# A two-layer decode step: layer 1's FFN gate and up products formed as rows, the last down product formed as rows on top of x, and more unread products between the layers

## The chip, the cores and the metric

The kernel runs on one core of a Trainium2 chip. The core has five engines with queues of their own: TensorE (matrix products, results to the PSUM banks), VectorE, ScalarE, GpSimd and SyncE (which here issues all transfers from HBM to SBUF). They run at the same time and wait for each other only through semaphores. The metric is the device time of one execution in microseconds (us); lower is better. Three runs of the kernel before took 645.3, 645.9 and 646.07 us, so the median is 645.9 us.

## The reference, cut to what matters

Two identical layers act on 4 sequences with one new token each. The weights and the caches are the same ones in both layers, so each layer needs all of the K and V cache.

```python
B, Sq, D = 4, 1, 512;  Hq, Hkv, Sk, Dh = 32, 8, 8192, 128;  F = 1792

def _A_ref(x, k_cache, v_cache, wq, wo):            # attention with 4 query heads per KV head
    q = (x @ wq).reshape(B, Sq, Hq, Dh).transpose(0, 2, 1, 3)
    k = jnp.repeat(k_cache, 4, axis=1);  v = jnp.repeat(v_cache, 4, axis=1)
    scores = jnp.einsum("bhqd,bhkd->bhqk", q, k) * (Dh ** -0.5)
    o = jnp.einsum("bhqk,bhkd->bhqd", _softmax(scores), v)
    return o.transpose(0, 2, 1, 3).reshape(B, Sq, Hq * Dh) @ wo

def _B_ref(x, w_gate, w_up, w_down):                # SwiGLU FFN
    return (_silu(x @ w_gate) * (x @ w_up)) @ w_down

x = x + _A_ref(_layernorm(x), ...);  x = x + _B_ref(_layernorm(x), ...)    # layer 1
x = x + _A_ref(_layernorm(x), ...);  x = x + _B_ref(_layernorm(x), ...)    # layer 2
```

K and V are 128 MiB together, in bfloat16.

## The kernel before, in words

**Units and slots.** The cache is cut into 32 units per layer, one for each sequence and KV head. K of a unit is 2 MB and so is V. SBUF has eight slots of this size; a transfer for a later unit is issued as soon as the unit that held the slot is done with it (`finished`, `pump`), all on SyncE's queue. Most units come as one transfer; those around the border between the layers come in quarters of 512 KB (`part`). K and V of the last three units of layer 1 stay in six slots and are used first in layer 2. In the meantime the other two slots (6 and 7) and a small extra area hold the FFN weights: w_gate (4 pieces of 448 KB), w_up (4 pieces, read once and kept for layer 2), w_down (7 pieces of 256 KB, one for each pair of 128 rows).

**Attention of a unit.** VectorE turns K in 32x32 blocks (`turn`), TensorE forms the scores in 8 blocks of 4 products of 256 columns (`scores`). Then five steps wait in a list `line` and are put between other work at estimated distances: `max_p` (VectorE), `max_t` (TensorE transpose, VectorE maximum, ScalarE copy), `exps` (TensorE broadcast of the maximum, ScalarE exponential), `turn_p`, `total`. `values` then multiplies by V, 16 products of 512 columns that go to four column groups of TensorE (lines 598 to 604). The last unit of a layer takes another form (`block_last`), eight blocks of 8 products of 32 columns, each waiting for its quarter of V. At the end of a KV head `out_proj` multiplies by wo and `add_to_x` adds to x. The scores, V products and softmax steps of the next or previous units are interleaved in the order in which Python calls them; each engine executes its own queue strictly in that order (`T.tape`).

**The border.** After the last unit of layer 1: `center` (the norm: sums by a product with ones, subtraction, squares), then `ffn(False)`, then `center` again, `qmul` (q of layer 2's first head), `qcast`, `qpick`, `place_q` and the first scores. All on x of 128 partitions by 16 columns, so every step is short and hands over between TensorE and VectorE.

**The FFN before.** w_gate and w_up are multiplied as weights: for each of 4 pieces (kt), 14 products with a 128x128 block as the stationary operand and 4 columns of x, repeated to 32, as the moving one (lines 782 to 789). The deviation of the norm comes in the middle of the gate. `gr`, `eg`, `gw` form silu on 128x56 (lines 793 to 799), and `hT` multiplies by up (line 800). w_down goes the same way, 14 x 4 products (lines 807 to 810). In layer 1, SyncE gets the first three K quarters of layer 2 (into slot 6) after the gate products, and four more after the second, sixth, tenth and last group of w_down, as the weights are used up (lines 790 to 792 and 811 to 817).

**The first unit of layer 2.** Its K is in a kept slot. After every second of its eight score blocks the slot's quarter is free and a V quarter of a later unit is issued into it (`quarter`, lines 559 to 563). So these transfers wait for TensorE's scores.

**The end.** Layer 2's FFN reads x plus the down product into `xn` (line 819). Four transposes on TensorE bring it to rows, ScalarE and VectorE copy one half each, and SyncE writes the 4 KB of output (lines 909 to 921).

**Unread products.** `warm(n, k)` (line 693) issues products of a wq block with itself, n pieces of 256 columns, into a bank that nobody reads. They depend on nothing late and fill time in which TensorE would wait.

Of the kernel before, what the change touches and what calls it, by code (L numbers as in the profile page):

```python
# [5 lines left out]
ACTF = mybir.ActivationFunctionType  # L6
# [139 lines left out]
def bass_interleave_layers__gqa_block_cached__swiglu_ffn__decode_kernel(  # L146
# [18 lines left out]
    P = 128  # L165
# [25 lines left out]
    with ExitStack() as es:  # L191
# [61 lines left out]
        def bank(k):  # L253
            return ps[:, k * BANKF:(k + 1) * BANKF]
# [162 lines left out]
        def part(it, s, a, b, sem_):  # L417
            kind, L, u = it
            assert (L, u) in fours
            n = NB // NQ  # L420
            w, m = n * TB * Dh, S // NQ
            src = (A_k_cache if kind == "K" else A_v_cache)[u % B, u // B, :, :]
            T.dma("sp", [(kv[:, s, q * w:(q + 1) * w], runs(src[q * m:(q + 1) * m, :])) for q in range(a // n, b // n)],
                  sem_, writes=[f"s{s}.{k}" for k in range(a, b)])

        def place(it, s):
            assert items[issued[0]] == it
            slot_of[it] = s
            issued[0] += 1
# [151 lines left out]
        def values(L, u):  # L581
            g, b = unit_gb(u)
            bk = OBK[turn_of[u]]
            def begin():
                flush(line, u)
                flush(after, turn_of[u])
# [5 lines left out]
            def block(i):  # L592

                if i == 0:
                    begin()
                s = slot_of["V", L, u]
                v = kv[:, s, :].rearrange("p (q t d) -> p t q d", t=TB, d=Dh)
                for t in range(TB):
                    j = t % NA
                    c0 = t * QB + i * NV * REP  # L600
                    T.pe(bank(bk)[j * QB:j * QB + NV * REP, :], pT[:, turn_of[u], c0:c0 + NV * REP],
                         v[:, t, NV * i:NV * (i + 1), :],
                         reads=[f"s{s}.{NV * i + k}" for k in range(NV)] + [f"pT{turn_of[u]}"], writes=[f"pb{bk}"],
                         sig=(t == TB - 1), start=(i == 0 and t == j), stop=(i == 1 and t >= TB - NA))
                if i == 1:
                    end()
# [158 lines left out]

        def ffn(last):
            gb, ub = OBK
            gT = bank(gb)[:, 0:FO * B]
            uT = bank(ub)[:, 0:FO * B]
            fb = lambda ap: ap.rearrange("p (f b) -> p f b", b=B)  # L770
            rb = rstd[:].unsqueeze(1).to_broadcast([P, FO, B])
            ks = items[ends[0] + 1:ends[0] + 3]
            n = NB // NQ
            w6 = KT * F // (TB * Dh) // n * n
            for (w_sb, wname, bk) in (([wg_sb[:, k, :] for k in range(KT)], "wg", gb), (wu_sb, "wu", ub)):
                out = bank(bk)[:, 0:WIDE // B * FO * B].rearrange("p (r f b) -> p f r b", f=FO, b=B)
# [13 lines left out]
                if bk == gb and not last:  # L790
                    place(ks[0], NKEEP)
                    part(ks[0], NKEEP, 0, w6, sem_p[0])
            T.op("dve", lambda e: e.tensor_tensor(fb(gr), fb(gT), rb, ALU.mult),
                 reads=[f"pb{gb}", "rstd"], writes=["gr"])
            T.op("act", lambda e: e.activation(eg, gr, ACTF.Exp, scale=-1.0), reads=["gr"], writes=["eg"])
            T.op("dve", lambda e: e.tensor_tensor(fb(gw), fb(gr), rb, ALU.mult), reads=["gr", "rstd"], writes=["gw"])
# [3 lines left out]
            T.op("dve", lambda e: e.tensor_tensor(hT, eg, uT, ALU.mult), reads=[f"pb{ub}", "eg"], writes=["hT"])  # L800
            out = bank(OUTB)[:, 0:WIDE // B * XB].rearrange("p (r n b) -> p n r b", n=KT, b=B)
            for fo in range(FO):
                if not last:
                    warm(2 if fo % 2 == 0 else 0)
                elif fo in (0, FO - 4, FO - 2):
                    warm(3 if fo == 0 else 1)
                for nt in range(KT):
                    T.pe(out[:, nt, :, :], wd_sb[:, fo, nt * P:(nt + 1) * P], few(hT[:, fo * B:(fo + 1) * B]),
                         start=(fo + nt == 0), stop=(fo == FO - 1 and nt == KT - 1),
                         reads=["hT"] + at_w["wd", fo // 2], writes=[f"pb{OUTB}"], sig=(nt == KT - 1 and fo % 2 == 1))  # L810
                if not last and (f1 - f0 + (fo + 1) * D) % (n * TB * Dh) == 0:
# [6 lines left out]
            if last:  # L818
                T.op("dve", lambda e: e.tensor_tensor(xn[:], xT[:], bank(OUTB)[:, 0:XB], ALU.add),
                     reads=["x", f"pb{OUTB}"], writes=["xn"])  # L820
            else:
                add_to_x()


        def roll(name):
# [57 lines left out]
        for L in range(2):  # L883
            turn_of.update((u, i % 2) for i, u in enumerate(unit_order[L]))
            rl_of.update((u, i % CYCLE) for i, u in enumerate(unit_order[L]))
            center(2 * L)
            first = unit_order[L][0] // B
            qmul(first)
            warm(L)
            qcast()  # L890
            qpick()
            warm(L)
            place_q(unit_order[L][0], "dve", ob4, [f"pb{OUTB}"])
            qkeep()
# [12 lines left out]
            ffn(L == 1)  # L907

        warm(2)
        for i, (k, eng, copy) in enumerate(((LNB, "act", lambda e, a, b: e.activation(a, b, ACTF.Copy)),  # L910
                                            (TOT, "dve", lambda e, a, b: e.tensor_copy(a, b)))):
            a, n = i * D // 2, KT // 2
            for kt in range(i * n, (i + 1) * n):
                T.pe(bank_bf(k)[0:B, kt * P:(kt + 1) * P], xn[:, kt * B:(kt + 1) * B], ident,
                     is_transpose=True, start=True, stop=True,
                     reads=["xn", "ident"], writes=[f"pb{k}"], sig=(kt == (i + 1) * n - 1))
            T.op(eng, lambda e: copy(e, xio[:, a:a + D // 2], bank_bf(k)[0:B, a:a + D // 2]), reads=[f"pb{k}"],
                 writes=[SCR[i]])
# [33 lines left out]
```

## Time and profile before

| what | value |
|---|---|
| median of three runs | 645.9 us |
| the profiled execution, its own time | 645.87 us |
| its span, first to last instruction | 644.1 us |
| busy: TensorE products, VectorE, ScalarE, GpSimd | 512.3, 448.8, 119.2, 19.3 us |
| mean granted clock of TensorE | 0.907 |
| bytes read from HBM | 273.42 MB |
| w_up's four pieces, when the products that wait for them start | 340.76, 341.83, 342.92, 344.00 us |
| layer 1's hT written, its last w_down pair started | 344.56, 348.39 us |
| layer 2's first scores | 351.51 us |
| output issued | 642.52 us |

The span is 1.8 us shorter than the time, which also holds what lies before the first and after the last instruction. Busy times of different engines lie beside each other and don't add up. A product's row includes the time in which its results drain from the array, so products that follow each other overlap in the rows. "Granted clock" is the share of TensorE's full clock that it was given in a stretch; 0.50 means that every product streams at half speed. The DMA share is the mean share of time in which the 16 DMA engines had a packet in work.

### The profile page before, as it was taken

Reading aid. Unit: us, or ns where it says so; the run is one execution under the profiler, and the core shown is the slowest. Engines: PE = TensorE matmul, PEld = TensorE weight load, DVE = VectorE, ACT = ScalarE, POOL = GpSimd, SP = SyncE. Lnnn points to the kernel's source line nnn. Section 1 sums busy time; section 2 is a strip of 40 time slices with the busy share of each in tenths; the row PEclk is TensorE's granted clock in tenths of the full one; section 3 lists DMA queues with packets and bytes.
Section 4 is the critical chain, followed back from the end, with each engine's and each line's share of the span. In section 5 each row is a group of like instructions: output and inputs, shape, how many; then the busy total and the mean of one; then the engine's idle time right before and its main releaser. Section 6 shows DMA issues by size and latency. Waiting matters only on the chain.

```text
span 644.1 us, 13095 instructions
## 1 busy us (share of the span) xinstructions
PE 512.3 (80%) x5088; PEld 333.1 (52%) x5113; DVE 448.8 (70%) x1105; ACT 119.2 (19%) x396; POOL 19.3 (3%) x73
## 2 busy tenths in 40 slices
PE   1657796877968877696988888989978878888887
PEld 1424464544535644454655655656555545555555
DVE  2646666866866866868763739889776776768783
ACT  0111121211211211211221222122221221111221
POOL 0000000000000000000000000000000000000000
PEclk9976789987999798889899989899798799869899
DMA  8999999999999999999999999999999999999996
GB/s 356 425 446 418 431 434 440 428 423 444 432 427 436 440 427 425 438 433 429 433 418 420 399 442 422 437 428 433 433 429 436 429 436 431 436 431 429 428 426 289
DMA packets 12744, 273.76 MB, mean 425 GB/s; under 512 B 3048, under 2 KB 3056, under 8 KB 3056
## 3 DMA queue, kind: packets, MB, share of 16 engines
q1 hardware_dynamic: 12720, 273.44, 99.1%
q8 instruction: 16, 0.26, 0.2%
q14 instruction: 8, 0.07, 0.0%
HBM read 273.42 MB, written 0.00 MB: 425 GB/s over the span
## 4 chain that ended last, share of the span: by engine, by line
DMA 63%; PE 19%; DVE 13%; SPq 2%; issue 1%; ACT 1%; DVEq 0%; POOL 0%; POOLq 0%
DMA kvf<-in_A_k_cache_dram 48%; PE ps L99 19%; DMA kvf<-in_A_v_cache_dram 11%; DVE kvf L117 8%; DMA kvf<-in_B_w_down_dram 3%; DVE acc L117 2%; SPq L135 2%; DVE one L117 1%; DVE pT L117 1%; DVE m L117 1%; ACT pb L117 0%; DVE oT L117 0%; DVEq L867 0%; ACT acc L117 0%; DVE qg L117 0%
## 5 line engine op out<-in xcount | busy, mean ns | idle before, releaser
L117 DVE STREAM_TRANSPOSE kvf<-kvf 128x512 f32<-128x512 f32 x488 | 322.5, 685 | 85.4 <-DMA kvf<-in_A_k_cache_dram 85.4
L99 PE MATMUL ps<-kvf,zq 128*128 128x256 bf16 x2048 | 314.7, 295 | 17.6 <-DVE kvf L117 12.3
L99 PEld LDWEIGHTS ps<-kvf,zq 128*128 128x128 bf16 x2048 | 196.1, 107 | 80.3 <-DVE kvf L117 30.0
L117 ACT ACTIVATE pb<-m 1x128 f32<-1x128 f32 x64 | 19.7, 308 | 438.6 <-DVE m L117 438.6
L99 PE MATMUL ps<-kvf,pT 128*16 128x512 bf16 x992 | 66.8, 391 | 11.5 <-DVE rl L117 6.9
L117 DVE SCALAR_TENSOR_TENSOR acc<-ps,own,acc 128x128 f32<-128x128 f32 x186 | 65.1, 350 | 6.2 <-ACT acc L117 1.5
L99 PE MATMUL ps<-identf,one 128*1 128x128 f32 x64 | 17.5, 274 | 50.3 <-DVE one L117 50.1
L99 PEld LDWEIGHTS ps<-identf,one 128*1 128x1 f32 x64 | 5.1, 80 | 78.5 <-DVE one L117 75.4
L99 PEld LDWEIGHTS ps<-kvf,pT 128*16 128x16 bf16 x992 | 19.3, 89 | 41.0 <-issue 21.4
L117 DVE TENSOR_REDUCE one<-ps 128x1 f32<-128x256 f32 x64 | 26.0, 406 | 18.3 <-PE ps L99 18.0
L99 PE MATMUL ps<-head,acc 128*128 128x4 f32 x124 | 23.9, 263 | 16.1 <-DVE acc L117 16.1
L117 ACT ACTIVATE pb<-ps,one,rstd 128x256 bf16<-128x256 f32 x64 | 36.1, 564 | 2.1
L99 PEld LDWEIGHTS ps<-head,acc 128*128 128x128 f32 x124 | 21.7, 218 | 28.0 <-DVE acc L117 27.0
L487 POOL TENSOR_TENSOR zq<-scr,quad 128x64 bf16<-128x64 bf16 x62 | 18.2, 293 | 600.3 <-PE ps L99 473.7
L99 PEld LDWEIGHTS ps<-one,pb 1*128 1x128 f32 x128 | 21.5, 209 | 27.0 <-ACT pb L117 21.8
L99 PE MATMUL ps<-one,pb 1*128 1x1 f32 x128 | 26.9, 277 | 9.5 <-ACT pb L117 9.5
L117 DVE RECIPROCAL rl<-ps 128x4 f32<-128x4 f32 x64 | 10.4, 162 | 33.3 <-PE ps L99 33.3
L99 PE MATMUL ps<-wq_sb 128*128 128x512 bf16 (+1 forms) x92 | 28.0, 369 | 2.7 <-issue 0.9
L117 DVE STREAM_TRANSPOSE pT<-pb 128x256 bf16<-128x256 bf16 x64 | 26.0, 407 | 4.4 <-ACT pb L117 4.3
L99 PE MATMUL ps<-xn,wq_sb 128*128 128x32 bf16 x270 | 19.8, 182 | 7.0 <-DMA wq_sb<-in_A_wq_dram 6.2
L99 PEld LDWEIGHTS ps<-o,wo_sb 128*128 (+1 forms) x256 | 20.4, 100 | 7.6 <-issue 3.5
L99 PE MATMUL ps<-o,wo_sb 128*128 128x32 bf16 x256 | 23.9, 181 | 0.1
(65 smaller groups left out, 245.4 us busy)
## 6 DMA issues: line engine op xcount, KB each, us to landing
kvf<-in_A_k_cache_dram SPq DMA_DIRECT2D x56, 2048.0 KB, 29.0
kvf<-in_A_v_cache_dram SPq DMA_DIRECT2D x56, 2048.0 KB, 32.6
kvf<-in_A_k_cache_dram SPq DMA_DIRECT2D x20, 512.0 KB, 9.0
kvf<-in_A_v_cache_dram SPq DMA_DIRECT2D x20, 512.0 KB, 11.2
wq_sb<-in_A_wq_dram SPq DMA_DIRECT2D x4, 1024.0 KB, 8.6
wo_sb<-in_A_wo_dram SPq DMA_DIRECT2D x8, 512.0 KB, 37.1
kvf<-in_B_w_gate_dram SPq DMA_DIRECT2D x8, 448.0 KB, 17.9
kvf<-in_B_w_down_dram SPq DMA_DIRECT2D x14, 256.0 KB, 18.5
```

What stands on the lines that cost most here:

```text
L99: return e.matmul(out, lhsT=lhsT if at is None else lhsT(place(at)), rhs=rhs, **kw)
L117: self.tape[engname].append((repr((name, args, kw)), lambda e, _: getattr(e, name)(*args, **kw), left, sig, None))
L135: ins = e.add_instruction(mybir.InstDMACopy(name=self.nc.get_next_instruction_name(), mode="Copy", queue="qSPDynamicHW", ins=e.lower_ap_dm ...
L487: T.op(eng, lambda e: e.tensor_tensor(dst, q4, m4_, ALU.mult), reads=keys_ + ["quad"], writes=["zq"])
```

## The change

It has four parts.

1. In `values`, when the next-to-last unit of a layer begins its V products, the list `line` is first run down to two entries. So `max_p`, `max_t` and `exps` of the last unit stand ahead of these products on every queue, in both layers.
2. `ffn(False)`: gate and up are formed as rows. For each piece, four products take x's 4 columns as the stationary operand and 448 columns of the weights as the moving one; the four go to the column groups at partitions 0, 32, 64 and 96 of one bank. When a matrix is done, VectorE turns the bank's 448 columns in 32x32 blocks from one PSUM bank into another (gate to the first score bank, up to the gate's bank), and `gT`, `uT` read every 32 columns' first four. The silu's first three operations (`gates`) stand right behind the gate's turn; the rest stands behind up's turn. Unread products: two pieces before each gate piece but the first, five before each up piece (before: three before all but up's first), six before the first w_down group (before: two).
3. `ffn(True)`: w_down is formed as rows. Two banks take 256 output columns each. Four products with the f32 identity put x there first, then for each of the 14 blocks two products with hT's 4 columns as the stationary operand and 256 columns of w_down as the moving one, at partitions 0 and 32. The addition, the four transposes and the unread products between w_down's groups are gone; ScalarE and VectorE copy the two row halves from PSUM.
4. At the border `center`, `qmul` and `qpick` of layer 2 get more unread products: four, three, two and three pieces where there were three, two, one and one.

```diff
             def block(i):
                 if i == 0:
+                    if u == unit_order[L][-2]:
+                        while len(line) > 2:
+                            line.pop(0)[2]()
                     begin()
...
-            gT = bank(gb)[:, 0:FO * B]
-            uT = bank(ub)[:, 0:FO * B]
+            gk, uk = (gb, ub) if last else (SBK[0], gb)
+            gT, uT = (bank(k)[:, 0:FO * (B if last else QB)].rearrange("p (f x) -> p f x", f=FO)[:, :, 0:B] for k in (gk, uk))
...
+            def gates():
+                T.op("dve", lambda e: e.tensor_tensor(fb(gr), gT, rb, ALU.mult),
+                     reads=[f"pb{gk}", "rstd"], writes=["gr"])
+                T.op("act", lambda e: e.activation(eg, gr, ACTF.Exp, scale=-1.0), reads=["gr"], writes=["eg"])
+                T.op("dve", lambda e: e.tensor_tensor(fb(gw), fb(gr), rb, ALU.mult), reads=["gr", "rstd"], writes=["gw"])
...
                 for kt in range(KT):
+                    if not last:
+                        if bk == gb and kt == KT // 2:
+                            deviation(zero_sb, "zero")
+                        if bk == ub or kt:
+                            warm(5 if bk == ub else 2)
+                        for j in range(NA):
+                            T.pe(bank(bk)[j * QB:j * QB + B, 0:F // NA], xn[:, kt * B:(kt + 1) * B],
+                                 w_sb[kt].rearrange("p (a j y) -> p a j y", j=NA, y=2 * QB)[:, :, j, :],
+                                 start=(kt == 0), stop=(kt == KT - 1), reads=at_w[wname] + [f"{wname}{kt}", "xn"],
+                                 writes=[f"pb{bk}"], sig=(j == NA - 1 and kt == KT - 1))
+                        continue
...
-                    if bk == ub and kt and not last:
-                        warm(3)
...
+                if not last:
+                    to = (SBK[0], gb)[bk == ub]
+                    T.op("dve", lambda e: e.transpose(bank(to)[:, 0:F // NA], bank(bk)[:, 0:F // NA].rearrange(
+                        "p (a i e) -> p a e i", e=2, i=QB)), reads=[f"pb{bk}"], writes=[f"pb{to}"])
+                    if bk == gb:
+                        place(ks[0], NKEEP)
+                        part(ks[0], NKEEP, 0, w6, sem_p[0])
+                        gates()
+            if last:
+                gates()
             T.op("dve", lambda e: e.tensor_scalar(eg, eg, 1.0, None, op0=ALU.add), reads=["eg"], writes=["eg"])
             T.op("dve", lambda e: e.reciprocal(eg, eg), reads=["eg"], writes=["eg"])
             T.op("dve", lambda e: e.tensor_tensor(eg, gw, eg, ALU.mult), reads=["gw", "eg"], writes=["eg"])
...
+            if last:
+                rows = [bank(k)[i * QB:i * QB + B, 0:D // 2] for i, k in enumerate((OUTB, STEP))]
+                for kt in range(KT):
+                    i, j = kt // (KT // 2), kt % (KT // 2)
+                    T.pe(rows[i][:, j * P:(j + 1) * P], xT[:, kt * B:(kt + 1) * B], identf[:], start=(j == 0), stop=False,
+                         reads=["x", "ident"], writes=[f"pb{(OUTB, STEP)[i]}"], sig=False)
+                warm(1)
+                for fo in range(FO):
+                    for i in range(2):
+                        T.pe(rows[i], hT[:, fo * B:(fo + 1) * B], wd_sb[:, fo, i * D // 2:(i + 1) * D // 2],
+                             start=False, stop=(fo == FO - 1), reads=["hT"] + at_w["wd", fo // 2],
+                             writes=[f"pb{(OUTB, STEP)[i]}"], sig=(fo == FO - 1))
+                return rows
...
-                if not last:
-                    warm(2 if fo % 2 == 0 else 0)
-                elif fo in (0, FO - 4, FO - 2):
-                    warm(3 if fo == 0 else 1)
+                warm(6 if fo == 0 else 2 if fo % 2 == 0 else 0)
...
-            center(2 * L)
+            center(3 * L)
...
-            warm(L)
+            warm(2 * L)
...
-            warm(L)
+            warm(3 * L)
...
-        warm(2)
...
+        T.op("act", lambda e: e.activation(xio[:, 0:D // 2], rows[0], ACTF.Copy), reads=[f"pb{OUTB}"], writes=[SCR[0]])
+        T.op("dve", lambda e: e.tensor_copy(xio[:, D // 2:D], rows[1]), reads=[f"pb{STEP}"], writes=[SCR[1]])
```

More of the change, by code (lines that the diff above doesn't have):

```diff
@@ L789, in ffn @@
                              sig=(fo == FO - 1 and kt == KT - 1))
[L790 to L796, printed above, removed]
+                if not last:
[8 more added lines that the diff above has]
+                gates()
             T.op("dve", lambda e: e.tensor_scalar(eg, eg, 1.0, None, op0=ALU.add), reads=["eg"], writes=["eg"])
@@ L799, in ffn @@
             T.op("dve", lambda e: e.tensor_tensor(eg, gw, eg, ALU.mult), reads=["gw", "eg"], writes=["eg"])
-            T.op("dve", lambda e: e.tensor_tensor(hT, eg, uT, ALU.mult), reads=[f"pb{ub}", "eg"], writes=["hT"])
+            T.op("dve", lambda e: e.tensor_tensor(fb(hT), fb(eg), uT, ALU.mult), reads=[f"pb{uk}", "eg"], writes=["hT"])
+            if last:
[11 more added lines that the diff above has]
+                return rows
             out = bank(OUTB)[:, 0:WIDE // B * XB].rearrange("p (r n b) -> p n r b", n=KT, b=B)
             for fo in range(FO):
-                if not last:
-                    warm(2 if fo % 2 == 0 else 0)
-                elif fo in (0, FO - 4, FO - 2):
-                    warm(3 if fo == 0 else 1)
+                warm(6 if fo == 0 else 2 if fo % 2 == 0 else 0)
                 for nt in range(KT):
@@ L810, in ffn @@
                          reads=["hT"] + at_w["wd", fo // 2], writes=[f"pb{OUTB}"], sig=(nt == KT - 1 and fo % 2 == 1))
-                if not last and (f1 - f0 + (fo + 1) * D) % (n * TB * Dh) == 0:
+                if (f1 - f0 + (fo + 1) * D) % (n * TB * Dh) == 0:
                     i = (f1 - f0 + (fo + 1) * D) // (n * TB * Dh) - NQ
@@ L817, in ffn @@
                         part(ks[1], NKEEP + 1, (i - 1) * n, i * n, sem_p[1 + i])
[L818 to L822, printed above, removed]
+            add_to_x()
         def roll(name):
@@ L906, in bass_interleave_layers__gqa_block_cached__swiglu_ffn__decode_kernel @@
             center(3)
-            ffn(L == 1)
-        warm(2)
[L910 to L918, printed above, removed]
+            rows = ffn(L == 1)
+        T.op("act", lambda e: e.activation(xio[:, 0:D // 2], rows[0], ACTF.Copy), reads=[f"pb{OUTB}"], writes=[SCR[0]])
+        T.op("dve", lambda e: e.tensor_copy(xio[:, D // 2:D], rows[1]), reads=[f"pb{STEP}"], writes=[SCR[1]])
         T.wait_res("sp", reads=SCR)
```

## The prediction

> **What bounds the kernel now.** First the page: the DMA row and the queue's share.
>
> ```profile
> DMA  8999999999999999999999999999999999999996
> q1 hardware_dynamic: 12720, 273.44, 99.1%
> HBM read 273.42 MB, written 0.00 MB: 425 GB/s over the span
> ```
>
> One queue keeps the 16 DMA engines busy for 99.1% of the span. No product can finish before its bytes are there, so an edit to a compute engine can change the time in two ways only: by letting the queue run dry, or by changing what follows the last byte. I looked for both.
>
> For the first, the stages around the border between the layers (columns: stretch, its length, then busy PE, PEld, DVE, ACT, POOL, granted clock, DMA share, GB/s):
>
> ```profile
> 344.80:348.30 3.50, 3.26 (x53) 1.75 (x54) 0.00 (x0) 0.00 (x0) 0.00 (x0) 1.00 1.08 442
> 348.30:351.70 3.40, 2.70 (x49) 1.61 (x50) 1.48 (x9) 0.15 (x1) 0.00 (x0) 1.00 0.98 414
> 351.70:355.10 3.40, 3.40 (x19) 2.46 (x18) 1.90 (x3) 2.20 (x4) 0.00 (x0) 0.50 1.01 424
> 355.10:358.50 3.40, 2.90 (x27) 2.25 (x25) 1.47 (x3) 0.00 (x0) 0.29 (x1) 1.00 0.94 352
> ```
>
> The clock is 0.50 for exactly the 3.4 us in which layer 2's first scores run, after 3.4 us of short work (norm, q). Right after, the DMA drops to 352 GB/s. From 354 to 362 the same view gives 381 GB/s against 429 in an undisturbed 10 us (590 to 600): 8 x (1 - 381/429) = 0.90 us of transfer lost. SyncE's timeline and the DMA issues (size, then us to landing), asked for in narrow windows, show why:
>
> ```profile
> 340.61 8.65 SPq L135 DMA_DIRECT2D kvf<-in_A_k_cache_dram  x7
> 353.58 2.18 SPq L135 DMA_DIRECT2D kvf<-in_A_v_cache_dram  x2
> 355.81 0.60 SPq L135 DMA_DIRECT2D kvf<-in_A_k_cache_dram  x1
> ```
>
> ```profile
> kvf<-in_A_k_cache_dram SPq DMA_DIRECT2D x1, 512.0 KB, 8.2
> ...
> kvf<-in_A_v_cache_dram SPq DMA_DIRECT2D x1, 512.0 KB, 4.6
> ...
> kvf<-in_A_v_cache_dram SPq DMA_DIRECT2D x1, 512.0 KB, 4.8
> ```
>
> The seventh K quarter (issued 348.79) lands 8.2 us after its issue, at 357.0. The first V quarter waits for the first scores and is issued at 353.58; it lands 4.6 us later, at 358.2, just in turn (one quarter, 0.52 MB at 429 GB/s, is 1.22 us). The second, 1.7 us behind it because the scores run at half clock, is issued at 355.29 and lands after 4.8 us, at 360.1, where its turn was 359.4. So 4.6 us is what a transfer takes when nothing is queued ahead, and these issues are too late for the queue.
>
> For the second way, the chain that ended last:
>
> ```profile
> 639.51 1.59 PE ps L99 x50
> 641.11 0.01 issue
> 641.12 0.38 PE ps L99 x8
> 641.50 0.02 issue
> 641.52 0.18 DVE xn L117
> 641.70 0.04 issue
> 641.75 0.40 PE ps L99 x4
> 642.15 0.02 issue
> 642.17 0.28 DVE scr L117
> ```
>
> The 8 products at 641.12 are w_down's last pair; in the timeline their weight load idles 0.20 us until that transfer has landed. Its issue was at 624.93 and its landing takes 16.1 us: 641.07. After that byte: products, add x, four transposes, two copies, and SyncE issues the output at 642.52: 1.45 us.
>
> **The change part by part.** The sum is made against the profiled execution: span 644.1, time 645.87, as good as the median (645.9).
>
> *Tail, w_down as rows.* Removed behind the last landing: 641.50 to 642.15, that is add and transposes, 0.65 us. Added: copies now read 256 f32 of PSUM, where DVE's CAST rows give 141 ns for 16 columns and 191 for 64, so 1.04 ns a column and 0.39 us for 256 (was 0.28); ACT's was 0.37 and stays about that. So -0.65 + 0.11, or -0.54. The last pair is 4 products of 256 columns in two column groups, 2 x 0.107 + 0.17 to drain (a 128-column bf16 product shows 218 ns, of which 53 stream) = 0.38, like the 0.38 it replaces. That takes two things. Groups must overlap: 16 P.V products of 512 columns in four groups take 1.04 us (row "kvf,pT", 625.94), serial it would be 3.4, so they do. And PE must have caught up: the four identity products (f32, two instructions each as all f32 products here; 128 columns take 0.107 by the f32 transposes' 274 ns against 218 for bf16, plus 0.05) are 8 x 0.107 = 0.85 us from 638.85, the one unread product 0.11, twelve steps of rows 12 x 0.11: 641.1, just there. Bounds: -0.65 (no dearer copy) and +1.0 (groups serial: 28 x 0.107 = 3.0 us from 639.8, so 643.0 in place of 641.5, less 0.54). I take -0.54, nearest to the P.V row.
>
> *Tail, softmax steps of the last unit moved ahead of the next-to-last P.V.* Its max, transpose and row broadcast now precede those 16 products; the broadcast starts at 627.85 when ACT is done, not 628.46, and the products lose 0.5 us while the chain gains 0.6. The work that hides it: V's last quarter and w_gate land up to 636.7 (issued 618.11, 18.6 us). I cost it at nothing; if TensorE were late at the end it would be worth up to 0.6. At the end of layer 1 the same, hidden by w_up and w_down.
>
> *Border, gate and up as rows.* 56 products of 32 columns per matrix (gate: 338.76 to 340.53) become 16 of 448 columns in four groups: 4 x 0.19 = 0.76, plus 3 x 0.21 unread, plus the deviation 0.2: done at 340.5 as before, so the first three K quarters still go out at 340.6. TensorE then waits for w_up (340.76, 341.83, 342.92, 344.00); five unread pieces, 0.53, fit into each 1.08. New on VectorE: two transposes of 128x448 f32, by the row of 128x512 (685 ns) 0.62 each; bounds 0.58 (448 at 1.04 ns plus 0.11) to 0.75.
>
> The second one stands ahead of four older operations on VectorE's queue, shown here as they are now:
>
> ```profile
> 341.10 0.19 DVE L117 TENSOR_SCALAR scr<-scr 128x56 f32<-128x56 f32 x1
> 341.33 0.50 DVE L117 RECIPROCAL scr<-scr 128x56 f32<-128x56 f32 x1
> 341.87 0.22 DVE L117 TENSOR_TENSOR scr<-scr 128x56 f32<-128x56 f32 x1
> 344.56 0.21 DVE L117 TENSOR_TENSOR scr<-scr,ps 128x56 bf16<-128x56 f32 x1 [2.48 <-PE ps L99]
> ```
>
> Today three of them are over 2.5 us before up is. Now up's rows end at 344.37, the transpose at 345.0, the three at 346.0, hT at 346.3 in place of 344.77: 1.5 us later. w_down's seven pairs then go at TensorE's pace, 0.43 a pair (344.82 to 345.25), not the DMA's 0.63: the last starts at 346.3 + 6 x 0.43 = 348.9 in place of 348.39. So 0.5 us of the 1.5 comes through to the norm and the first scores, 352.0 in place of 351.5. The later K quarters go out up to 1.5 us late (345.22 becomes 346.8) and land 353.3 or later, with over 4.6 in hand: nothing.
>
> *Border, unread products.* Five more pieces of 256 columns between 348.4 and 351.5, each put where TensorE waits for VectorE: no delay. A column takes 0.42 ns at full clock (512-column unread products follow at 0.21 us); counted so, the streamed columns fill 0.35 of 348.3 to 351.7 today; five times 0.107 makes 0.50. Stretches with 0.40 to 0.42 (334 to 345) were followed by full clock, so I expect full clock here. Scores then take 0.11 each: the first V quarter goes out at 352.0 + 8 x 0.11 + 0.35 (deviation, drain) = 353.25, the second at 354.2. Needed for their turns: 353.6 and 354.8. The queue does not run dry: -0.83 (of the 0.90: 0.66 before the second V quarter's landing and 0.17 before a later one's). Bounds: -0.90, and, with the clock still down, +0.5 for the 0.5 us of lateness.
>
> On the clock the Trainium skill ("TensorE: Matmul & The Clock Gate", Part 1) says that it follows free-running windows of 3.4 us, halved after an idle one. The trace agrees with the length; a phase that differs by run, as it says, would let the same kernel gain or lose up to these 0.8 us.
>
> **Sum:** 645.87 - 0.54 - 0.83 = 644.5.
>
> **The rivals.**
> A, as summed: 644.5, own range 644.1 to 645.0.
> B, the border gains nothing: hT's lateness eats what the clock gives, or the clock drops anyway. For it: 1.5 us new wait is worked out, not guessed. Against: 1.0 of it fits into waits for w_down. 645.87 - 0.54 = 645.3.
> C, the rows of the tail are not overlapped, or TensorE has not caught up: -0.83 + 1.0 = 646.0. Against: the P.V row.
> D, slower: the clock falls in the new idle stretch ahead of hT (345.0 to 346.3), and w_down's seven pairs run at half clock, 0.70 (8 x 0.034 + 0.43) in place of 0.43: they end 7 x 0.70 = 4.9 after 346.3, at 351.2 instead of 348.8. First V quarter at 356.0, 2.4 late, the second 0.5 more: 2.9 lost less 0.83 lost already, less 0.54: 647.4. It decides once that quarter is issued after about 355.7. Against: w_up's five pieces before and six behind put the filled share of any 3.4 us there at 0.43 or more by my count.
> E, more than summed: border 0.90, tail 0.65 and 0.3 us of the softmax turns out to count: 644.0.
> F, TensorE empties at each change between full-width and column-group products. The tail has two such changes, around the unread product; at the 0.17 us of a drain they take 0.34 of its gain: 644.8 (layer 1's gate, with seven, ends 1.2 later, ahead of a wait for w_up). Against: at 351.03 a full-width unread product starts while q's column-group products, begun at 350.79 for 0.30 us, still run to 351.09. The Trainium skill's page "TensorEngine Tiling (Array Packing)", Key Properties, has it as a rule that changing the tiling mode drains the engine; this trace does not agree.
>
> **How the numbers follow.** A 0.55, B 0.17, C 0.08, D 0.07, E 0.08, F 0.05. A measurement tells about 0.2% from no change, so faster is below 644.6, slower above 647.2. A lies across that bound, a little over half of it below (0.30 faster, 0.25 same); E faster, B, C and F same, D slower: 0.38, 0.55, 0.07. The range 643.9 to 646.0 holds A, B, C, F and E's greater part; D is left out.
>
> **What would show it.** Right: clock 1.00 at the first scores, V quarters about 1 us apart, over 420 GB/s from 354 to 362, and the output issued about 0.9 us after w_down's last landing. hT near 346.3 shows the order on VectorE. Wrong: clock 0.50 at w_down or the first scores, a first V quarter after 353.6, row products that take 3 us, or a w_down landing that is not 0.8 us earlier than 641.07.

## The result: 648.75 us, half a per cent slower

The changed kernel takes 648.75 us (median of 20 runs, 646.01 to 651.9); the kernel before took 645.57 us beside it (20 runs, 645.11 to 646.27). The ratio is 1.0054, with a 95% interval of 1.0045 to 1.0062. So it is slower, by 3.2 us, where 644.5 us were forecast. The profiled execution took 651.18 us with a span of 649.4; it is one of the slowest of its 20, so its losses are larger than the median's. Its span is 5.3 us above that of the profiled execution of before (644.1). 0.6 of this stood there ahead of the border (V of the next-to-last unit of layer 1 lands at 330.99 in place of 330.39), 3.6 were added from there to w_down's last landing (645.31 in place of 641.07), and 1.1 behind it. One later execution of the kernel before, in the group that e9 to e12 are measured against, took 959.04 us and counts in no ratio.

### The page of the kernel after

```profile
DMA  8999999999999999999999999999999999999996
GB/s 351 423 440 420 441 429 430 439 428 434 430 432 438 430 434 430 432 436 430 432 415 352 369 434 432 431 429 432 432 436 432 432 432 432 434 434 430 423 429 264
q1 hardware_dynamic: 12720, 273.44, 98.6%
HBM read 273.42 MB, written 0.00 MB: 421 GB/s over the span
```

The same bytes, at 421 GB/s in place of 425. The loss of transfer rate is in one place: slices 21 to 23 (one is 16.2 us, so 325 to 373 us) show 415, 352 and 369 GB/s where the neighbours have about 430. That is the border. (The last slice falls from 289 to 264; that is the longer end, behind the last bytes.) The stretches of it (start and end, length, busy PE, PEld (TensorE's weight loads), DVE, ACT, POOL, granted clock, DMA share, GB/s):

```profile
329.50:334.10 4.60, 3.08 (x40) 1.24 (x40) 1.61 (x6) 1.77 (x6) 0.00 (x0) 1.00 0.99 413
334.10:340.90 6.80, 6.05 (x94) 4.30 (x94) 2.40 (x10) 0.37 (x1) 0.00 (x0) 0.50 1.00 419
340.90:344.30 3.40, 3.37 (x39) 1.57 (x38) 1.01 (x7) 0.23 (x1) 0.00 (x0) 1.00 0.99 410
...
348.00:352.00 4.00, 2.86 (x37) 1.34 (x38) 1.68 (x5) 0.00 (x0) 0.00 (x0) 1.00 0.83 326
354.00:362.00 8.00, 7.42 (x85) 5.33 (x85) 4.68 (x14) 2.35 (x4) 0.29 (x1) 1.00 0.92 317
```

Half clock is there, but not where the prediction looked for it: it lies at 334.1 to 340.9, in the softmax and V products of layer 1's last unit, while the DMA still runs. At the first scores (after 356) the clock is 1.00, as forecast. The DMA falls off most from 348 on.

### The wait at 333: VectorE's order

Before, VectorE around layer 1's last maximum (start, length, operation, and in brackets the idle time before it and who ended it):

```profile
330.16 0.28 DVE L117 TENSOR_REDUCE m<-ps 1x4 f32<-1x128 f32 x1 [0.75 <-PE ps L99]
331.06 1.12 DVE L117 SCALAR_TENSOR_TENSOR acc<-ps,own,acc 128x128 f32<-128x128 f32 x3 [0.62 <-ACT acc L117]
332.81 0.45 DVE L117 STREAM_TRANSPOSE pT<-pb 128x256 bf16<-128x256 bf16 x1 [0.62 <-ACT pb L117]
...
337.83 0.18 DVE L117 TENSOR_REDUCE vs<-xT 128x4 f32<-128x16 f32 x1
```

and TensorE's weight load for the sum of `acc`, from the same execution:

```profile
332.24 0.30 PEld L99 LDWEIGHTS ps<-head,acc 128*128 128x128 f32 x2 [0.54 <-DVE acc L117]
```

And after, VectorE again, followed by three lines of TensorE's products and the same weight load:

```profile
331.27 0.28 DVE L117 TENSOR_REDUCE m<-ps 1x4 f32<-1x128 f32 x1 [0.75 <-PE ps L99]
333.34 0.45 DVE L117 STREAM_TRANSPOSE pT<-pb 128x256 bf16<-128x256 bf16 x1 [1.79 <-ACT pb L117]
333.71 1.08 DVE L117 SCALAR_TENSOR_TENSOR acc<-ps,own,acc 128x128 f32<-128x128 f32 x3
...
341.82 0.18 DVE L117 TENSOR_REDUCE vs<-xT 128x4 f32<-128x16 f32 x1
```

```profile
331.95 0.38 PE L99 MATMUL ps<-one,pb 1*128 1x1 f32 x2 [0.71 <-ACT pb L117]
332.26 1.04 PE L99 MATMUL ps<-kvf,pT 128*16 128x512 bf16 x16
334.85 0.59 PE L99 MATMUL ps<-head,acc 128*128 128x4 f32 x2 [1.55 <-DVE acc L117]
```

```profile
334.85 0.50 PEld L99 LDWEIGHTS ps<-head,acc 128*128 128x128 f32 x2 [2.06 <-DVE acc L117]
```

The broadcast of the maximum does come early, 0.68 us behind the maximum's start (331.27 to 331.95); before it came at 331.41, 1.25 behind it. But three additions into `acc`, left over from an earlier unit, have changed places with the transpose `pT` of the last one. Before, they filled VectorE's wait for ScalarE's exponential. After, `pT` stands ahead, VectorE idles 1.79 us for that exponential with the additions queued behind it, and TensorE, whose queue has the sum of `acc` (`head,acc`) ahead of the last unit's products, waits 2.06 us where it waited 0.54. The code says why. `advance` serves the list `line` before the list `after`. When the new lines run, `exps` is the only step of theirs left in `line`; calling it early makes `turn_p` the first entry, so the next `advance` issues `turn_p` ahead of `own_others`, which waits in `after`.

From the maximum's start to the first sum of layer 1's norm it is 7.67 us before (330.16 to 337.83) and 10.55 after (331.27 to 341.82). In layer 2 it is 7.66 and 8.81, there at full clock.

### What the lateness does to the queue

The border's later steps, VectorE and then SyncE's queue (SPq):

```profile
348.98 0.67 DVE L117 STREAM_TRANSPOSE ps<-ps 128x448 f32<-128x448 f32 x1 [2.58 <-PE ps L99]
349.55 0.17 DVE L117 TENSOR_SCALAR scr<-scr 128x56 f32<-128x56 f32 x1
349.76 0.50 DVE L117 RECIPROCAL scr<-scr 128x56 f32<-128x56 f32 x1
350.30 0.22 DVE L117 TENSOR_TENSOR scr<-scr 128x56 f32<-128x56 f32 x1
350.55 0.21 DVE L117 TENSOR_TENSOR scr<-scr,ps 128x56 bf16<-128x56 f32 x1
```

```profile
345.27 8.92 SPq L135 DMA_DIRECT2D kvf<-in_A_k_cache_dram  x7
357.72 1.36 SPq L135 DMA_DIRECT2D kvf<-in_A_v_cache_dram  x2
```

hT is written at 350.76, not at the forecast 346.3, and the first V quarter goes out at 357.72, not at 353.25. The fourth K quarter goes out at 351.21, only 1.42 us before the third has landed, and the landings of the fourth and fifth come 2.45 and 2.53 us behind their predecessors, where quarters that are queued in time land 1.22 to 1.24 apart: 2.5 us lost. The second V quarter's takes 2.98: another 1.75.

The end, of the kernel after (w_down's last pair landed at 645.31):

```profile
645.59 1.69 PE L99 MATMUL ps<-kvf,scr 128*4 128x256 bf16 x28
647.32 0.37 ACT L117 ACTIVATE scr<-ps 4x256 bf16<-4x256 f32 x1 [3.28 <-PE ps L99]
647.35 0.42 DVE L117 CAST scr<-ps 4x256 bf16<-4x256 f32 x1 [1.99 <-PE ps L99]
647.84 0.27 SPq L942 DMA_DIRECT2D out_dram<-scr  x1
```

All 28 row products run after the last landing, because hT of layer 2 comes at 645.37. The output goes out 2.53 us behind that landing; it was 1.45 before and forecast as 0.9. The chain that ended last has no transfer in its last stretch:

```profile
639.70 1.29 PE ps L99 x19
640.99 0.04 issue
641.03 6.30 PE ps L99 x155
647.33 0.02 issue
647.35 0.42 DVE scr L117
```

### The profile page after: what moved, and what is told of

It reads as the page before. It is cut to its first block, busy times and chain, and to the rows that moved or that the text cites. A ratio compares the mean times of both kernels' runs of the same rounds, so it can differ in the third digit from the quotient of the medians.

```text
span 649.4 us, 12928 instructions
## 1 busy us (share of the span) xinstructions
PE 522.8 (81%) x5018; PEld 335.5 (52%) x5018; DVE 450.2 (69%) x1106; ACT 119.3 (18%) x396; POOL 19.3 (3%) x73
## 4 chain that ended last, share of the span: by engine, by line
DMA 61%; PE 20%; DVE 15%; issue 2%; ACT 1%; SPq 0%; DVEq 0%; POOL 0%; POOLq 0%
DMA kvf<-in_A_k_cache_dram 53%; PE ps L99 20%; DVE kvf L117 9%; DMA kvf<-in_A_v_cache_dram 9%; DVE acc L117 3%; DVE one L117 1%; ACT pb L117 1%; DVE pT L117 1%; DVE m L117 1%; SPq L135 0%; DVE scr L117 0%; DVE oT L117 0%; ACT one L117 0%; DVEq L897 0%; DVE ps L117 0%
## 5 line engine op out<-in xcount | busy, mean ns | idle before, releaser
L99 PEld LDWEIGHTS ps<-kvf,zq 128*128 128x128 bf16 x2048 | 198.3, 108 | 80.5 <-DVE kvf L117 27.8
L99 PE MATMUL ps<-kvf,pT 128*16 128x512 bf16 x992 | 68.5, 399 | 12.1 <-DVE rl L117 8.1
L99 PE MATMUL ps<-wq_sb 128*128 128x512 bf16 (+1 forms) x126 | 38.6, 396 | 0.0
L117 DVE TENSOR_REDUCE one<-ps 128x1 f32<-128x256 f32 x64 | 26.0, 406 | 15.6 <-PE ps L99 15.4
L99 PEld LDWEIGHTS ps<-rsm,one 128*128 128x128 f32 x128 | 22.1, 215 | 4.3 <-ACT rsm L117 2.5
```

Source lines behind the costliest of these rows:

```text
L99: return e.matmul(out, lhsT=lhsT if at is None else lhsT(place(at)), rhs=rhs, **kw)
L117: self.tape[engname].append((repr((name, args, kw)), lambda e, _: getattr(e, name)(*args, **kw), left, sig, None))
```

## The experiments

Twelve kernels ran; each computes everything that the reference does. The median of the kernel before in the same group of runs is given each time (645.17 to 645.58), because it differs a little from group to group; ratios are to it, with 95% intervals. The first question was which part costs; the next, whether it is the lateness itself or the clock that falls in the new wait.

**e1: the change without the moved softmax steps.**

```diff
-                    if u == unit_order[L][-2]:
-                        while len(line) > 2:
-                            line.pop(0)[2]()
```

> The changed kernel without its first part (the last unit's softmax steps stay where they were in both layers). Theory S (the moved steps put the last unit's turn of p ahead of the three accumulations of an earlier unit on VectorE; TensorE idles 2.0 us, the clock falls, the FFN comes 4 us late and the K quarters with it): 644.4 to 645.2 us, layer 1's norm within 0.3 us of where it was relative to the landing of the next-to-last V, clock 1.00 there. Theory D (hT's lateness behind up's turn and the clock there are the cause): still 647 to 649. Theory R (rows with changes of tile width slow TensorE): still 647 to 649, with gate and up taking over 0.9 us a piece.

Measured: 645.95 us (11 runs, 644.71 to 647.69) against 645.58, 1.0007 [0.9997, 1.0016]. That lies between the two forecasts. The other three parts together are no loss that can be told, and 2.8 us below the whole change. So the moved steps cost about 2.8 of it.

**e2: the moved steps alone, put into the kernel before.** The same lines, added.

> The kernel before with the first part of the change alone. S: slower than before, 646.7 to 648.5: 1.1 us from the end of layer 2, where nothing follows that could hide it, and 0 to 1.8 at the border, where the old FFN order leaves VectorE and TensorE about 1 us in hand. TensorE idle 2 us behind the next-to-last V products in both layers. D and R: 645.0 to 645.9, as before.

Measured: 646.92 us (11 runs) against 645.58, 1.0017 [1.0007, 1.0026]: +1.3 us. The wait for `acc` is the same 2.06 us. So the part is slow by itself, but less so beside the old FFN, where hT had time in hand: in its profile (646.2 us) hT comes 14.6 us after the landing of V of the next-to-last unit, 14.4 before, and the queue loses nothing there. What can be read is at the end, 1.92 us from w_down's last landing to the output, in place of 1.45; where the rest of the 1.3 lies, this execution doesn't show.

**e3: the whole change, with the additions called ahead of the V products too.**

```diff
                         while len(line) > 2:
                             line.pop(0)[2]()
+                        while len(after) > 1:
+                            after.pop(0)[2]()
```

> The changed kernel, all four parts, with one thing more: when the steps are moved, the pending accumulations on VectorE are put out too, ahead of the turn of p. S: 644.2 to 645.0, as without the move or up to 0.3 less; the idle 2 us are gone. A rival within S (the moved exps themselves do the harm, by holding the next-to-last V products back 0.5 us): 646 or more. D and R: 647 to 649.

Measured: 645.5 us (11 runs, 644.69 to 648.53) against 645.58, 1.0006 [0.9993, 1.0018]. One restored order on one engine gives back about 3 us, though the time is 0.5 above the range forecast for it. VectorE in e3:

```profile
330.54 0.28 DVE L117 TENSOR_REDUCE m<-ps 1x4 f32<-1x128 f32 x1 [0.75 <-PE ps L99]
331.45 1.12 DVE L117 SCALAR_TENSOR_TENSOR acc<-ps,own,acc 128x128 f32<-128x128 f32 x3 [0.62 <-ACT acc L117]
332.61 0.45 DVE L117 STREAM_TRANSPOSE pT<-pb 128x256 bf16<-128x256 bf16 x1
```

The additions are back in the wait for the exponential, and the norm's first sum comes 7.32 us after the maximum's start, 0.35 less than before the change. That this is a gain of the moved steps is not shown: e8, which has the old order, also shows 7.32 in layer 1. And e10 against e4, below, shows none of it in the time.

**e4: e1, and silu's three operations moved into `gates`**, so that they stand ahead of up's turn on VectorE (`tensor_scalar`, `reciprocal` and the product with `gw`).

```diff
                 T.op("dve", lambda e: e.tensor_tensor(fb(gw), fb(gr), rb, ALU.mult), reads=["gr", "rstd"], writes=["gw"])
+                T.op("dve", lambda e: e.tensor_scalar(eg, eg, 1.0, None, op0=ALU.add), reads=["eg"], writes=["eg"])
+                T.op("dve", lambda e: e.reciprocal(eg, eg), reads=["eg"], writes=["eg"])
+                T.op("dve", lambda e: e.tensor_tensor(eg, gw, eg, ALU.mult), reads=["gw", "eg"], writes=["eg"])
```

> The changed kernel without its first part and with silu's remaining three operations ahead of up's turn on VectorE, so hT waits for the turn alone. S: 644.2 to 645.0, at most 0.5 below the run without the first part, since 1.0 of hT's 1.5 us was in hand. D: this one drops to 645 and the one without the first part stays above 647.

Measured: 644.83 us (11 runs, 644.47 to 646.07) against 645.58, 0.9991 [0.9982, 1.0]; 1.1 us below e1. Its hT follows up's turn at once:

```profile
344.61 0.67 DVE L117 STREAM_TRANSPOSE ps<-ps 128x448 f32<-128x448 f32 x1 [1.54 <-PE ps L99]
345.30 0.21 DVE L117 TENSOR_TENSOR scr<-scr,ps 128x56 bf16<-128x56 f32 x1
```

```profile
354.00:362.00 8.00, 7.50 (x72) 5.18 (x70) 6.59 (x15) 1.52 (x5) 0.58 (x2) 1.00 1.01 416
```

and the eight microseconds that have 371 GB/s in e1, and 317 in the changed kernel, have 416. So the operations behind up's turn cost 1.1 us, not the 0.5 that the prediction let through.

**e5: e1, with 18 unread pieces ahead of w_down instead of 6**, so that TensorE doesn't idle while it waits for hT.

```diff
-                warm(6 if fo == 0 else 2 if fo % 2 == 0 else 0)
+                warm(18 if fo == 0 else 2 if fo % 2 == 0 else 0)
```

> The changed kernel without its first part, and with 18 unread pieces in place of 6 ahead of layer 1's first w_down group, so that TensorE works on in most of the 1.4 us in which it waits for hT; hT itself stays as late (about 1.5 us behind w_up's turn-around of before). Without the first part the kernel measured 645.95, with silu early 644.83. Theory C (the late hT costs by letting the clock fall in the wait, in some runs): median 644.6 to 645.2, highest run below 646.5. Theory L (the lateness itself costs): 645.6 to 646.3, spread as before, 644.7 to 647.7.

Measured: 645.98 us (11 runs, 644.69 to 647.12) against 645.43, 1.0007 [0.9998, 1.0015], the same as e1. The clock in that wait is not what costs there, which speaks against rival D at the place where the prediction had put it; what remains is that hT is late.

**e6: the whole change, with 14 unread pieces behind the next-to-last V products**, to fill the wait for `acc`.

```diff
                 if i == 1:
+                    if u == unit_order[L][-2]:
+                        warm(14, SBK[turn_of[u]])
                     end()
```

> The whole change, and 14 unread pieces behind the next-to-last unit's V products in both layers, in the time in which TensorE waits for VectorE's accumulations. If what the moved softmax steps cost is mostly the clock that falls in this wait: 646.0 to 647.0, and no half clock between 330 and 350. If it is the 1.1 us of lateness from the order on VectorE: 648 or more, as the whole change (648.75).

Measured: 647.88 us (5 runs, 646.82 to 648.66) against 645.43, 1.0033 [1.002, 1.0046]. The clock stays up:

```profile
334.10:337.50 3.40, 3.29 (x90) 2.75 (x88) 1.46 (x6) 0.17 (x1) 0.00 (x0) 1.00 0.97 407
337.50:340.90 3.40, 3.30 (x44) 1.62 (x39) 1.13 (x7) 0.00 (x0) 0.00 (x0) 1.00 1.01 418
```

From the maximum to the norm it is 8.81 us here, in place of 10.55. The time is 0.9 us below the changed kernel, and about 2 above e1, between the two expectations: by the medians the half clock is about a third of the 2.8 us, and the late additions alone are the larger part. With five runs, whose times overlap those of the changed kernel, the size of that third is not well known.

**e7: the whole change, with e4's move.**

> The whole change, with silu's remaining operations ahead of up's turn. The order of VectorE there measured 1.1 us without the first part. If the two orders act one after the other on the same chain: 647.0 to 647.8 (648.75 less 1.0 to 1.7). If either alone uses up the same reserve, and the moved steps come first: 648 or more.

Measured: 648.44 us (6 runs, 647.07 to 649.74) against 645.43, 1.0043 [1.0029, 1.0057]: 0.3 below the changed kernel, which is within the spread of both. By the medians, what was worth 1.1 in e4 is worth almost nothing here, but six runs between 647.07 and 649.74 can't exclude that it is worth 1.1 again. In this profile hT is written at 348.31, the first V quarter is issued at 355.26, and the queue runs dry, as it does in the changed kernel.

**e8: w_down as rows at the end, alone, in the kernel before.** The branch `if last:` with `rows` and the two copies.

> The kernel before with the third part of the change alone, layer 2's w_down as rows on top of x. By the working on record -0.54 us: 644.9 to 645.3 against 645.6, the output issued 0.9 to 1.0 us after w_down's last landing in place of 1.45. Rival (rows not overlapped, or TensorE late behind the identity products): 646.0 or more.

Measured: 644.81 us (11 runs, 644.7 to 646.42) against 645.43, 0.9996 [0.9988, 1.0005]: 0.62 less between the medians, where 0.54 was forecast, though the interval includes no change. The output goes out 0.98 us after w_down's last landing (640.38 to 641.36), in place of 1.45.

**e9: more unread products at the border, alone.**

```diff
-            center(2 * L)
+            center(3 * L)
...
-            warm(L)
+            warm(2 * L)
...
-            warm(L)
+            warm(3 * L)
```

> The kernel before with the fourth part alone, five more unread pieces at the border. If the half clock at layer 2's first scores, seen in the profile of before, is there in most runs, as the working on record took it: 644.7 to 645.0 (0.5 to 0.8 less). If it is a matter of the run, there in some and not in others: a median 0.1 to 0.4 less, the lowest runs as before (645.05) and the highest fewer.

Measured: 645.2 us (11 runs, 645.05 to 646.32) against 645.17, 1.0 [0.9991, 1.0009]. The gain of 0.83 is not there, nor the 0.1 to 0.4 that the other forecast named. e8 shows why: at the border it has the kernel before's own code, and this is its clock there.

```profile
348.30:351.70 3.40, 2.73 (x50) 1.66 (x49) 1.49 (x9) 0.37 (x1) 0.00 (x0) 1.00 1.01 429
351.70:355.10 3.40, 3.40 (x32) 2.77 (x30) 1.90 (x3) 1.98 (x4) 0.00 (x0) 1.00 1.00 419
```

The products ahead are as thin as in the profile of before (2.73 us busy, 2.70 there), yet the first scores run at 1.00. They do so in e2 and e12 too, which also have the old number of unread products there. So of four traced executions with that code one has the half clock that the prediction wanted to remove; it comes and goes with the execution.

**e10: all four parts, with both orders on VectorE mended (e3 and e4).**

> All four parts with both orders on VectorE mended: the pending accumulations ahead of the turn of p, and silu's operations ahead of up's turn. Theory S with lateness: 644.6 to 645.0, as the run with silu early and without the moved steps (644.83), few runs above 645.5; the moved steps then bring nothing or up to 0.2. If moving the steps costs anything but the order: 645.3 or more.

Measured: 644.8 us (11 runs, 644.62 to 645.9) against 645.17, 0.9992 [0.9983, 1.0001].

**e11: the end as rows and the unread products at the border, in the kernel before.**

> The kernel before with the third and fourth parts: w_down of layer 2 as rows, and the unread pieces at the border. Tail alone measured 644.81. 644.5 to 644.8, and if layer 1's rows bring nothing of their own, not above the runs that have them (644.83).

Measured: 644.73 us (11 runs, 644.62 to 645.45) against 645.17, 0.9992 [0.9983, 1.0001]. So gate and up as rows and the moved steps, even mended, add nothing to the rows at the end. e4, e8, e10 and e11 lie within about 0.1 us of each other; each is below the kernel before by 0.4 to 0.75 us, but the intervals reach to 1, so a gain over it is likely and not shown.

**e12: gate and up as rows, alone.**

> The kernel before with the second part alone, layer 1's gate and up as rows, turned by VectorE, silu's rest behind up's turn. By the runs so far (645.95 with parts two to four, less the tail's gain of 0.6 to 0.8): 646.3 to 647.0, and a wide spread. By the working on record (1.0 of 1.5 us in hand, 0.5 passed on): 645.6 to 646.1.

Measured: 646.43 us (12 runs, 645.17 to 648.95) against 645.17, 1.0018 [1.0008, 1.0028]: +1.3 us. This agrees with e4 against e1, by the other way round.

**The count.** From 645.57: the rows at the end −0.6 (e8), gate and up as rows +1.1 (e1 against e4) to +1.3 (e12), the moved steps +2.8 (the change against e1), the unread products at the border 0.0 (e9). That makes 648.9 to 649.1; measured is 648.75. This is no independent test of the 2.8, which is itself the difference of the change and e1; alone, in the kernel before, the moved steps cost 1.3 (e2), so what they cost depends on the parts beside them.

**How much of a product's lateness comes through.** In these profiles, by the issues and landings of the transfers: how long before the last K quarter's landing the first V quarter is issued, and by how much the four landings after that K quarter exceed 4 x 1.23 us.

| profile | hT written, after the landing of V of the next-to-last unit | first V quarter issued ahead of the last K quarter's landing | lost over the next four landings |
|---|---|---|---|
| e8 / e11 / e2 / e9 | 14.4 / 14.3 / 14.6 / 14.4 us | 4.17 / 4.18 / 4.19 / 4.18 us | 0.0 us |
| e4 / e10 | 15.5 / 15.4 | 4.10 / 4.18 | 0.0 |
| before (half clock at the scores) | 14.4 | 3.38 | 0.85 |
| e12 / e1 / e5 | 16.4 | 3.31 / 3.22 / 3.18 | 1.0 / 0.6 / 1.1 |
| e3 | 16.5 | 3.07 | 0.8 |
| e7 | 17.6 | 2.56 | 1.8 |
| after | 19.8 | 2.52 (and the K quarters late: 2.5 more) | 1.8 |
| e6 | 17.5 | 2.09 | 2.1 |

With 4.1 us in hand nothing is lost, with 3.4 or less 0.6 to 2.1 us. One microsecond of hT (e4 to e1) crosses that edge: hT 1.1 us later than in e8 costs nothing, 2.0 us later costs 0.6 to 1.1. At the same lead the loss differs by 0.5 us from one execution to the next, which may be a part of why the kernels near 3.3 scatter so much (e12 over 3.8 us, e11 over 0.8).

It is not all of it. The profiled execution of e12 (648.55 us) has its last landing 3.06 us behind that of e8. 0.66 of this stood there ahead of the border, about 0.7 were added from the border on, and 1.7 fall on a single transfer: w_down's last pair lands 2.34 us behind the pair before it (641.10 to 643.44), in e8 0.62 behind. In e12's DMA records one 16 KB instruction packet runs from 641.35 for 1.0 us, and the pair's last packet starts at 642.34, as it ends. So that time is not a price of the rows.

## Why the prediction was wrong, and where it was right

**The step that failed** is "softmax steps of the last unit moved ahead of the next-to-last P.V … I cost it at nothing", and its copy for layer 1. The prediction followed the moved steps themselves (maximum, transpose, broadcast) and had them right: the broadcast came 0.6 us earlier against the maximum. It did not follow what the move does to the work that stays: `line` is served before `after`, so `turn_p` moved up as well and the additions fell behind it. The price is a wait of 2.06 us on TensorE in place of 0.54, in both layers. 1.15 us of it are on the way to the norm at full clock (8.81 against 7.66 in layer 2), and 1.7 more in the profile of after at the half clock that came with it (10.55 against 8.81). The cover named for it, V's last quarter and w_gate landing up to 636.7, holds against TensorE being busy 0.5 us longer. It doesn't hold against the norm being late, because behind the norm lies a chain of short steps that no transfer shortens: in e4 it takes 7.25 us from the norm's first sum to the output (633.87 to 641.12; 0.33 of that is a wait for w_down), in the kernel after 7.05 (640.79 to 647.84). So a microsecond there, beyond that wait, goes straight to the end: 1.55 us of the loss in the profiled execution is read there (2.53 in place of 0.98).

**Border, unread products, −0.83: nothing came.** The reading of the half clock was right in itself, 0.85 us lost in that execution, though at w_down's last landing only 0.45 of it is left against e8 (641.07 against 640.38, of which 0.24 stood there ahead of the border). But one execution was taken for the kernel: the median of 20 runs is 645.57 and in one group 645.17, not 645.9, and e9 stays at 645.2. The prediction had a sentence that allowed this (a phase that differs by run) and gave it no rival of its own; rival B has the border gain nothing, but for other causes. Nor does the streamed share tell the two apart: e8's stretch is as thin as the one that the prediction counted at 0.35, and full clock follows. The Trainium skill's page "TensorE: Matmul & The Clock Gate", Part 1, has the windows run free of the kernel; these runs agree: at the border the same 2.06 us wait comes with half clock for 6.8 us in the profile of after and for 3.4 us in those of e2 and e7, and at the end of layer 2 with none in all three.

**hT late by 1.5, of which 0.5 comes through.** The mechanism was right, the order on VectorE is exactly the one drawn, and e4 shows it. Two terms were mis-sized. The first is the lateness: 2.0 us by the table (16.4 against 14.4), not 1.5. The gate's rows were to be "done at 340.5 as before", 1.8 us after their start; they take 2.4 (342.75 to 345.17; in e12 339.20 to 341.62), and an up piece with its unread ones takes 0.94 (345.75 to 346.69) where 0.72 was reckoned (0.53 + 0.19). So up's rows end 1.0 us after w_up's last landing in e1, not 0.4. The second is the reserve. The prediction took 4.6 us as what a quarter needs from issue to landing when nothing is queued ahead, and so 353.6 and 354.8 as early enough for the first two V quarters. That figure doesn't hold: in the changed kernel the first V quarter landed 3.76 us after its issue (357.72 to 361.48), and in e12 the second, issued 4.9 us ahead of its turn, landed 1.0 us late. By the table 3.4 us ahead of the K quarter is already too late, 4.1 is not. So 1.1 us came through.

**The end as rows, −0.54: right.** −0.62 in e8. The copies took 0.37 and 0.42 (forecast 0.37 and 0.39), the column groups overlap: 28 products in 1.69 us where serial ones were put at 3.0, so rival C fell. The eight products with the identity took 0.61, not 0.85.

**Rival D** named the mechanism, a clock that falls while TensorE waits for VectorE, and a side, slower; but it put it at hT. There e5 finds no cost. It fell one step earlier, in a wait that the prediction had not seen. **Rival F** had a grain of truth in layer 1: each group of four rows of 448 columns takes 0.29 us until the next product starts (342.75 to 343.04), where 448 columns stream in 0.19, and the two unread pieces behind take 0.32 (343.04 to 343.36), where two of 0.107 are 0.21. About 0.1 us more than the columns take at each change between column groups and full width, then. That this is the array emptying is argued, not shown; it agrees with the rule of the Trainium skill's "TensorEngine Tiling (Array Packing)", Key Properties, that a change of tiling mode drains the engine; the prediction had rejected it by one row of short q products. At the end of layer 2 its share is too small to be seen beside −0.62.

**Still open:** why a V quarter that is issued late lands later than its turn, and which one: the first comes in turn in before, e1, e5, e12 and the changed kernel, and 0.4 to 0.9 us late in e3, e6 and e7. And how the 2.8 us divide between the border and the end of layer 2, which no run separates.

## What to carry to other kernels

When a step is called earlier, write down for each engine what stood between its old place and its new one, and who was waiting for that: here three additions of an earlier unit, which nobody had meant to move, cost 2.8 us, and putting them back returned about 3. In a kernel that lives on one transfer queue, price lateness in how far ahead of the queue the next issue stands; as long as that reserve is there a late product is free, and beyond it a part comes through (here 0.6 to 1.1 of 2.0 us). A stall seen in a single profile is not yet a property of the kernel: the same code without it may be the more frequent case.

## What the runs showed of the hardware that was not expected

A wait of 2.06 us on TensorE came with 6.8 us at a granted clock of 0.50 in one execution, with 3.4 us in two others, and at the end of layer 2 of the same three with none. Groups of four column-group products between full-width ones took 0.29 us where their columns stream in 0.19, and the full-width pair behind them 0.32 in place of 0.21. The time from issue to landing of a 512 KB transfer on a nearly empty queue is not one figure: 4.6 us in the kernel before, 3.8 in the changed one. First V quarters issued 3.1 to 3.4 us ahead of the landing before them went with 0.6 to 1.1 us lost over four landings, those issued 4.1 us ahead with none. And one 16 KB instruction packet, 1.0 us long, went with a last weight transfer 1.7 us late (e12).
